# Both products of a mixture-of-experts step as seven block products, the weights' low halves by adding DMAs, and an issue order computed from a graph

## The chip, the core and the metric

The kernel runs on one core of a Trainium2 chip. The metric is the device time of one execution in microseconds (us); the time before is the median of three runs.

## What is computed

A local and global attention makes x (1536 tokens of 512 numbers). Two mixture-of-experts layers follow, both of one form, the first with 4 experts, the second with 8:

```python
for e in range(E):
    h = np.maximum(x @ w1[e], 0.0)          # 512 -> 1024
    out += p[:, e:e + 1] * (h @ w2[e])      # 1024 -> 512
```

In the first layer p comes from an input, normalised over the experts. In the second it comes from `x @ w_gate` by eight rounds of normalising rows and columns (a Sinkhorn iteration), so it is known only some time after that layer has begun.

## The kernel before, in words

**Steps.** The tokens are two blocks of 768, the hidden width of an expert is cut into units of 256: 48 units (16 in the first layer, 32 in the second) times 2 blocks make 96 steps. A step makes a 256 x 768 piece of h from w1 and x (first product), and multiplies it with a 256 x 512 piece of w2 (second product). Every number is a pair of a rounded high half and a low half (`hi`, `lo`), and a product is three matmuls: hi·hi, hi·lo, lo·hi.

**First product** (`product`, L485). It is cut into quadrants and made from seven block products in place of eight, by combinations S1 to S4 of the quadrants of w1 and T1 to T4 of those of x (A11, B21 and so on are the quadrants themselves). A block product is 2 x 3 matmuls of 384 columns, so a step has 42. Partial sums are copied out of PSUM by ACT (L519, L524, L528), later ones added by DVE (L514); ACT makes the rectified high half (L493), DVE the low half (L498).

**Second product** (`g2_tile`, L561 to L563). For each of 6 tiles of 128 tokens, 6 matmuls of 512 columns run into one PSUM bank, 36 in a step. DVE multiplies with p and adds to `acc` in one operation (L581). The result lies with tokens on partitions, so between the layers PE transposes it (`turn_pieces`, L591), and stores of the last step go straight out of `acc` (L585).

**Weights.** One load brings 512 KB of w1 or w2 into `scr`. ACT copies the high halves (L124), POOL subtracts to the low halves (L127) and forms the sums S1 to S4 (L163). There are two sets of weight tiles, a and b.

**Order.** The whole program is written out by hand: `weave` takes pieces of the step's products, the previous step's tiles, the next weights and extra work in the order of strings as STEADY. SP issues all DMAs. Step 0's first product lies inside the attention, as do the first weights (`filler`).

Of the kernel before, what the change touches and what calls it, by code (L numbers as in the profile page):

```python
# [18 lines left out]
def local_global_attention_moe_moe(  # L19
# [46 lines left out]
    ps_x = ctx.enter_context(tc.tile_pool(name="ps_x", bufs=3, space=PSUM))  # L66
    ps_m = ctx.enter_context(tc.tile_pool(name="ps_m", bufs=5, space=PSUM))
# [4 lines left out]
    p1 = const.tile([P, NTT, E1], F32, name="p1")  # L72
# [5 lines left out]
    pp = const.tile([P, NTT, E2], F32, name="pp")  # L78
    rs = const.tile([P, NTT], F32, name="rs")
# [3 lines left out]

# [5 lines left out]

    def new_x(pool, b, c):
        return [pool.tile([P, NOP, HB], F32R, name=f"x{n}{b}{c}") for n in ("hi", "lo")]

    def new_weights(pool, s):
        return {  # L100
            "w1hi": pool.tile([P, NOP, KH, P], F32R, name=f"w1hi_{s}"),
            "w1lo": pool.tile([P, NOP, KH, P], F32R, name=f"w1lo_{s}"),
            "w2hi": pool.tile([P, FC, DM], F32R, name=f"w2hi_{s}"),
            "w2lo": pool.tile([P, FC, DM], F32R, name=f"w2lo_{s}"),
        }

    def new_h(pool, s):
        return [pool.tile([P, FC, BLK], F32R, name=f"{n}_{s}") for n in ("hhi", "hlo")]

    def new_acc(pool, b):  # L110
        return [pool.tile([P, DM], F32, name=f"acc{b}_{t}") for t in range(TPB)]

    xop = {(0, 0): new_x(xp, 0, 0), (0, 1): new_x(xp, 0, 1), (1, 0): new_x(xp, 1, 0)}
    acc = new_acc(xp, 0)
    wsets = [new_weights(xp, "a"), None]
    hsets = [new_h(xp, "a"), None]
# [3 lines left out]
    NU = len(units)  # L120

# [6 lines left out]


    stage = {}  # L130

    def scratch(a, n=KD * FU):
        t = xp.tile([P, 2 * BLK], F32, name="scr", tag="scr", bufs=3)
        return t[:, 0:n].rearrange("x (a c) -> x a c", a=a)

    def load_w1(u):
        layer, e, f = units[u]
        t = stage[u, 1] = scratch(KD)
        w1 = (w1a, w1b)[layer]
        nc.sync.dma_start(  # L140
            out=t, in_=w1[e, :, f * FU:(f + 1) * FU].rearrange("(c p) f -> p c f", p=P)
        )

    def load_w2(u):
        layer, e, f = units[u]
        t = stage[u, 2] = scratch(FC, KD * FU)
        w2 = (w2a, w2b)[layer]
        nc.sync.dma_start(
            out=t, in_=w2[e, f * FU:(f + 1) * FU, :].rearrange("(c p) d -> p c d", p=P)
        )  # L150

# [725 lines left out]
```

## Time and profile before

| | |
|---|---|
| median of three runs | 1630.58 us (1629.75 to 1632.85) |
| the profiled execution's own time | 1632.92 us |
| its span in the trace | 1631.1 us |
| busy share of the span: PE, DVE, ACT, POOL | 98%, 55%, 36%, 35% |
| granted TensorE clock | 0.995 of full speed |

A matmul's recorded duration overlaps the next matmul's; what a matmul costs is read from one start to the next. The same holds for DVE and ACT, whose next operation may start before the recorded end of the one before.

### The profile page before, as it was taken

What the parts mean: (1) busy time and instruction counts of PE and PEld (TensorE: products, weight loads), DVE (VectorE), ACT (ScalarE), POOL (GpSimd) and SP (SyncE); (2) the same over time, 40 slices, a digit from 0 to 9 for tenths busy, and PEclk for the clock granted to TensorE, in tenths of its full rate; (3) what the DMA queues carried; (4) which work ended last, traced back from release to release, by engine and by line L of the source; (5) the groups of instructions that cost most, each with busy time, mean ns of one, the idle gap of its engine ahead of it and who ended that gap; (6) DMA issues with size and microseconds to landing.
All of it is one profiled execution on the core that took longest, in us unless ns stands there. A gap on an engine that the chain in (4) does not pass through costs nothing.

```text
span 1631.1 us, 21762 instructions
## 1 busy us (share of the span) xinstructions
PE 1603.1 (98%) x8515; PEld 1442.1 (88%) x8515; DVE 890.5 (55%) x1524; ACT 580.7 (36%) x1281; POOL 566.0 (35%) x648
## 2 busy tenths in 40 slices
PE   8989999999999998999999999999999999999999
PEld 7878998998999887889999899899998998999987
DVE  7875545545555464377555554554555545545555
ACT  5753333323323345323333333332332333333331
POOL 2743324323333454233432432432333333243240
PEclk9999999999999999999999999999999999999999
DMA  8811110110110001010110011011011011011002
GB/s 190 195 48 44 36 38 26 39 39 27 39 39 27 26 27 52 13 40 27 39 39 27 27 38 39 27 39 39 27 39 39 27 40 39 27 39 39 27 13 78
DMA packets 85032, 70.27 MB, mean 43 GB/s; under 512 B 36032, under 2 KB 71104, under 8 KB 84928
## 3 DMA queue, kind: packets, MB, share of 16 engines
q1 hardware_dynamic: 84928, 68.87, 14.1%
q8 instruction: 67, 1.10, 0.3%
q14 instruction: 37, 0.30, 0.1%
HBM read 64.53 MB, written 3.15 MB: 41 GB/s over the span
## 4 chain that ended last, share of the span: by engine, by line
PE 92%; POOL 3%; DVE 2%; ACT 1%; issue 1%; DMA 0%; SPq 0%; DVEq 0%; POOLq 0%; ACTq 0%
PE px L485 36%; PE pm L561 16%; PE pm L562 16%; PE pm L563 16%; PE pz L485 6%; PE ps L377 1%; POOL xlo L127 1%; PE po L415 1%; POOL scr L603 1%; PE pa L405 0%; POOL scr L163 0%; PE pg L641 0%; ACT xhi L124 0%; DVE xfa L194 0%; POOL w1lo_a L127 0%
## 5 line engine op out<-in xcount | busy, mean ns | idle before, releaser
L581 DVE SCALAR_TENSOR_TENSOR acc<-pm,pp,acc 128x512 f32<-128x512 f32 x347 | 260.4, 751 | 186.7 <-PE pm L563 185.4
L127 POOL TENSOR_TENSOR w1lo_a<-scr,w1hi_a 128x512 fp32r<-128x512 f32 (+1 forms) x144 | 117.6, 837 | 320.2 <-ACT w1hi_a L124 317.1
L514 DVE TENSOR_TENSOR c<-pz,c 128x384 f32<-128x384 f32 x96 | 53.5, 557 | 315.5 <-PE pz L485 311.1
L127 POOL TENSOR_TENSOR w1lo_b<-scr,w1hi_b 128x512 fp32r<-128x512 f32 (+1 forms) x144 | 116.6, 831 | 280.9 <-ACT w1hi_b L124 272.8
L519 ACT COPY c<-px 128x384 f32<-128x384 f32 x96 | 46.1, 481 | 431.7 <-PE px L485 431.7
L485 PE MATMUL px<-xhi,w1hi_a 128*128 128x384 f32 x576 | 196.6, 341 | 3.1 <-ACT c L528 1.4
L485 PE MATMUL px<-xhi,w1hi_b 128*128 128x384 f32 x576 | 194.8, 338 | 2.2 <-ACT c L519 1.0
L485 PE MATMUL px<-xhi,w1lo_a 128*128 128x384 f32 x576 | 194.9, 338 | 0.0
L485 PE MATMUL px<-xlo,w1hi_a 128*128 128x384 f32 x576 | 194.3, 337 | 0.2 <-POOL xlo L127 0.2
L485 PE MATMUL px<-xhi,w1lo_b 128*128 128x384 f32 x576 | 193.8, 337 | 0.0
L485 PE MATMUL px<-xlo,w1hi_b 128*128 128x384 f32 x576 | 193.2, 335 | 0.0
L581 DVE SCALAR_TENSOR_TENSOR acc<-pm,p,acc 128x512 f32<-128x512 f32 x180 | 134.7, 750 | 99.6 <-PE pm L563 99.6
L163 POOL TENSOR_TENSOR scr<-scr 128x256 f32<-128x256 f32 x188 | 140.0, 745 | 11.0
L514 DVE TENSOR_TENSOR c<-px,c 128x384 f32<-128x384 f32 x192 | 106.9, 557 | 45.7 <-PE px L485 45.6
L561 PE MATMUL pm<-w2hi_a,hhi_a 128*128 128x512 f32 x312 | 122.0, 391 | 3.0 <-ACT acc L570 2.0
L561 PE MATMUL pm<-w2hi_b,hhi_b 128*128 128x512 f32 x312 | 122.2, 392 | 0.0
L563 PE MATMUL pm<-w2hi_a,hlo_a 128*128 128x512 f32 x312 | 122.2, 392 | 0.0
L562 PE MATMUL pm<-w2lo_a,hhi_a 128*128 128x512 f32 x312 | 122.0, 391 | 0.0
L562 PE MATMUL pm<-w2lo_b,hhi_b 128*128 128x512 f32 x312 | 122.0, 391 | 0.0
L563 PE MATMUL pm<-w2hi_b,hlo_b 128*128 128x512 f32 x312 | 121.9, 391 | 0.0
L127 POOL TENSOR_TENSOR w2lo_a<-scr,w2hi_a 128x512 fp32r<-128x512 f32 x48 | 61.7, 1306 | 167.9 <-ACT w2hi_a L124 165.9
L127 POOL TENSOR_TENSOR w2lo_b<-scr,w2hi_b 128x512 fp32r<-128x512 f32 x48 | 61.4, 1300 | 166.7 <-ACT w2hi_b L124 166.7
(155 smaller groups left out, 3456.8 us busy)
## 6 DMA issues: line engine op xcount, KB each, us to landing
scr<-in_moe_w_dram SPq DMA_DIRECT2D x96, 512.0 KB, 3.3
vs<-in_v_dram SPq DMA_DIRECT2D x16, 240.0 KB, 3.9
kn<-in_k_dram SPq DMA_DIRECT2D x16, 192.0 KB, 3.3
qn<-in_q_dram SPq DMA_DIRECT2D x16, 192.0 KB, 4.2
vn<-in_v_dram SPq DMA_DIRECT2D x8, 384.0 KB, 3.4
out_dram<-acc SPq DMA_DIRECT2D x12, 256.0 KB, 2.0
vs<-vb SPq DMA_DIRECT2D x8, 144.0 KB
vs<-in_v_dram SPq DMA_DIRECT2D x32, 24.0 KB, 3.7
```

Of the source, the lines that this page charges most:

```text
L127: lo_eng.tensor_tensor(out=lo, in0=src, in1=hi.bitcast(F32), op=ALU.subtract)
L163: sum_eng.tensor_tensor(out=out, in0=x, in1=y, op=op)
L377: nc.tensor.matmul(wide[:, tt], bd[i % 2][:, g * GT + tt].rearrange("x j q -> x (j q)"), kw[i][:, g * GT + tt], start=False, stop=True, sk ...
L415: nc.tensor.matmul(po[j * D:(j + 1) * D, tt * QT:(tt + 1) * QT], vs[i][:, g * GT + tt, j, :], aT[:, tt, j, :], start=True, stop=True,)
L485: nc.tensor.matmul(pm, w[l][:, a, c, :], r[:, x, :], start=first and i == 0, stop=i == n - 1, skip_group_check=True,)
L514: nc.vector.tensor_tensor(out=c, in0=pm, in1=c, op=ALU.add)
L519: nc.scalar.copy(out=c11, in_=px)
L561: nc.tensor.matmul(pm, hhi[:, c, ts], w["w2hi"][:, c, :], start=(c == 0), stop=False)
L562: nc.tensor.matmul(pm, hhi[:, c, ts], w["w2lo"][:, c, :], start=False, stop=False)
L563: nc.tensor.matmul(pm, hlo[:, c, ts], w["w2hi"][:, c, :], start=False, stop=(c == FC - 1))
L581: nc.vector.scalar_tensor_tensor(out=acc[T], in0=pm, scalar=scal, in1=acc[T], op0=ALU.mult, op1=ALU.add)
L603: eng.tensor_tensor(out=out, in0=x, in1=y, op=ALU.subtract)
```

## The change

**Second product.** It too is made from seven block products, of the quadrants of w2 and h and their combinations (`add_second`): per half of the 512 outputs seven block products of 3 matmuls of 384 columns, 42 matmuls in a step. The result lies with tokens on columns, like x. p can no longer be a factor per partition, so it is multiplied into h (`relu`, `PB` is a row of p copied to all partitions through DRAM). The partial results are kept in five accumulators per block and half (m1, m2, z, c12, c22), combined only at the layers' border (`add_turn`) and at the end (`add_out`), where PE now transposes. In the second layer's first expert p is not known yet: those 8 steps leave it out, and `add_scale` multiplies the accumulators later.

**Operands of the second product.** `add_hop` makes the seven combinations of h with four subtractions on DVE, seven high halves on ACT, six low halves on DVE and one on POOL.

**Weights.** w1 and w2 both get S1 to S4 (four sums of 256 columns on POOL each). The low halves are no longer subtracted: ACT writes the negative of the rounded number, and a DMA issued by POOL adds the number to it in SBUF (`accum_op`), three such DMAs for each unit's w1 and w2. The tiles of A11, A12, A22 exist twice, those of S1 to S4 once.

**Order.** Behind the attention every operation is put on a list with what it reads and writes and with a due time; `run_work` issues them by earliest possible start under the table of costs `SPAN`, and by due time among equals. DVE operations with two SBUF inputs and POOL's arithmetic are kept apart there (`port`). The blocks of a unit now always follow each other (b = 0, 1); before, they were exchanged at the border.

```diff
+    SLOT = {A22: 0, A11: 1, A12: 2, S1: 6, S2: 7, S4: 8, S3: 9}
+    NSL = 10
...
+    def slot(u, a):
+        return SLOT[a] + (3 * (u % 2) if SLOT[a] < 3 else 0)
...
-        for c in range(FC):
-            nc.tensor.matmul(pm, hhi[:, c, ts], w["w2hi"][:, c, :], start=(c == 0), stop=False)
-            nc.tensor.matmul(pm, hhi[:, c, ts], w["w2lo"][:, c, :], start=False, stop=False)
-            nc.tensor.matmul(pm, hlo[:, c, ts], w["w2hi"][:, c, :], start=False, stop=(c == FC - 1))
...
-    def relu_lo(S, f, t, c):
-        hhi, hlo = hsets[S[2] % 2]
-        sl = slice(t * HB, (t + 1) * HB)
-        nc.vector.scalar_tensor_tensor(
-            out=hlo[:, f, sl], in0=c, scalar=0.0, in1=hhi[:, f, sl].bitcast(F32),
-            op0=ALU.max, op1=ALU.subtract,
-        )
...
+    def relu(S, out, src, th):
+        if plain(S):
+            nc.scalar.activation(out=out, in_=src, func=AF.Relu)
+        else:
+            nc.vector.scalar_tensor_tensor(
+                out=out, in0=src, scalar=0.0, in1=PB[S[1]][:, th * HB:(th + 1) * HB],
+                op0=ALU.max, op1=ALU.mult,
+            )
...
+            for eng, ids in avail.items():
+                f = free.get(eng, 0.0)
+                for i in ids:
+                    t = max(f, at[i], port) if work[i][5] else max(f, at[i])
+                    key = (t, work[i][3], i)
+                    if best is None or key < best:
+                        best = key
+            t, _, i = best
...
+            aop(lambda: nc.scalar.copy(out=h, in_=src), rd, [key + ("hi",)], due, span)
+            aop(lambda: nc.scalar.mul(l, src, -1.0), rd, [key + ("lo",)], due, span)
+            op(
+                "POOL", "pd", rd, [key + ("lo",)], due + 0.05,
+                lambda: nc.gpsimd.dma_start(out=l, in_=src, accum_op=ALU.add),
+            )
+
+        group(slot(u, A22), 3, 0, wkey(kind, u, A22), start + 0.2, "a768")
...
+        group(6, 2, 0, wkey(kind, u, S1), start + LEAD2, "a512")
+        group(8, 2, 2, wkey(kind, u, S4), start + LEAD2 + 0.1, "a512")
...
+        def one(i, name, due):
+            hi, lo = hop[i][:, 0], hop[i][:, 1]
+            aop(lambda: nc.scalar.copy(out=hi, in_=q[name]), [name], [("hi", i)], due, "ah")
+            eng = "POOL" if i in LOPOOL else "DVE"
+            lo_op(eng, lo, q[name], hi, [name, ("hi", i)], [("lo", i)], due + 0.01)
+
+        def sub(o, x, y, due):
+            vop(lambda: vsub(q[o], q[x], q[y]), [x, y], [o], due)
+
+        one(B11, "q11", d)
+        sub("q12", "q12", "q11", d)
+        one(T1, "q12", d + 0.03)
+        sub("t2", "q22", "q12", d + 0.03)
+        one(T2, "t2", d + 0.1)
+        sub("t4", "t2", "q21", d + 0.1)
+        one(B21, "q21", d + 0.12)
+        one(T4, "t4", d + 0.15)
+        sub("q11", "t2", "q11", d + 0.15)
+        one(B22, "q22", d + 0.2)
+        one(T3, "q11", d + 0.25)
...
+            def fn(cols=cols):
+                s = slot(u, x)
+                for i, (l, r) in enumerate(((hi, 0), (hi, 1), (lo, 0))):
+                    nc.tensor.matmul(
+                        cut[bank], l[:, s, cols], hop[t][:, r],
+                        start=start and i == 0, stop=i == 2, skip_group_check=True,
+                    )
...
+        def copy(out, kout, src, kin, due):
+            aop(lambda: nc.scalar.copy(out=out, in_=src), [kin], [kout], due)
...
+            t, key, bk = acc[b, k, dc], ("acc", b, k, dc), ("bank", bank)
+            if key in fresh:
+                fresh.remove(key)
+                copy(t, key, cut[bank], bk, due)
+            else:
+                vop(lambda: vadd(t, cut[bank], t), [bk, key], [key], due, two=False)
...
+            add_first(n)
+            if b == 1 and u > 0:
+                add_weights(u, 2, n - LEAD)
+            if b == 1 and u + 1 < NU:
+                add_weights(u + 1, 1, n + 1 - LEAD)
+            add_second(n - 1)
+            if n == border:
+                add_turn(0, n + 0.5)
+            if n == border + 1:
+                add_turn(1, n + 0.5)
+            add_hop(n)
...
+            if n == border + 3:
+                add_sinkhorn(n + 0.6)
...
+            if n in (border + 9, border + 10):
+                i = n - border - 9
+                add_scale(i, xf[:, i], n + 0.5)
+        add_second(NS - 1)
...
+        add_out(0, NS + 0.5, stages[0:3], (0, 1, 2, 7))
+        add_out(1, NS + 1.5, stages, tuple(range(8)))
+        run_work()
```

**What the engines issue now.** PE, in the second layer's steady part, before: the first product of a step stands in one piece (`px`, `pz`), then the tiles of the previous step (`pm`).

```order
L485 MATMUL px<-xhi_83,w1hi_b 128x384
L485 MATMUL px<-xlo_84,w1hi_b 128x384
L485 MATMUL px<-xhi_83,w1lo_b 128x384
L561 MATMUL pm<-w2hi_a,hhi_b 128x512
L562 MATMUL pm<-w2lo_a,hhi_b 128x512
L563 MATMUL pm<-w2hi_a,hlo_b 128x512
```

PE at the corresponding place of the change; bank_1552 to 1554 are px, py, pz, bank_1555 to 1558 the second product's four banks, h_1562 to 1568 the operands B11, B21, B22, T1, T2, T3, T4 of the second product.

```order
L509 MATMUL bank_1552<-xlo_84,w1hi 128x384
L509 MATMUL bank_1552<-xhi_83,w1lo 128x384
L758 MATMUL bank_1556<-h_1562,w2hi 128x384 x2
L758 MATMUL bank_1556<-h_1562,w2lo 128x384
L758 MATMUL bank_1558<-h_1565,w2hi 128x384 x2
L758 MATMUL bank_1558<-h_1565,w2lo 128x384
L509 MATMUL bank_1553<-xhi_81,w1hi 128x384
L509 MATMUL bank_1553<-xlo_82,w1hi 128x384
L509 MATMUL bank_1553<-xhi_81,w1lo 128x384
L509 MATMUL bank_1553<-xhi_83,w1hi 128x384
L509 MATMUL bank_1553<-xlo_84,w1hi 128x384
```

Block products of the second product (3 matmuls, L758) now stand between those of the first (6 matmuls, L509).

DVE before, one step: three additions, four low halves, then six accumulations.

```order
L514 TENSOR_TENSOR c_8823<-pz,c_8823 128x384
L514 TENSOR_TENSOR c_8832<-px,c_8832 128x384
L498 SCALAR_TENSOR_TENSOR hlo_a<-c_8823,hhi_a 128x384
L514 TENSOR_TENSOR c_8840<-px,c_8840 128x384
L498 SCALAR_TENSOR_TENSOR hlo_a<-c_8832,hhi_a 128x384
L498 SCALAR_TENSOR_TENSOR hlo_a<-c_8840,hhi_a 128x384
L498 SCALAR_TENSOR_TENSOR hlo_a<-px,hhi_a 128x384
L581 SCALAR_TENSOR_TENSOR acc_0_1538<-pm,pp,acc_0_1538 128x512
L581 SCALAR_TENSOR_TENSOR acc_1_1539<-pm,pp,acc_1_1539 128x512
L581 SCALAR_TENSOR_TENSOR acc_2_1540<-pm,pp,acc_2_1540 128x512
L581 SCALAR_TENSOR_TENSOR acc_3_1541<-pm,pp,acc_3_1541 128x512
```

DVE of the change, about half a step of its 26 operations (q_94 to q_96 are quadrants of h, t_97 and t_98 their combinations, m, z and c the accumulators):

```order
L130 TENSOR_TENSOR z_1573<-bank_1556,z_1573 128x384
L130 TENSOR_TENSOR c_00_1575<-bank_1555,c_00_1575 128x384
L133 TENSOR_TENSOR q_94<-q_94,q_93 128x384
L133 TENSOR_TENSOR t_97<-q_96,q_94 128x384
L523 SCALAR_TENSOR_TENSOR q_95<-bank_1552,pb_1589 128x384
L130 TENSOR_TENSOR c_00_1577<-bank_1558,c_00_1577 128x384
L130 TENSOR_TENSOR m_01_1572<-bank_1556,m_01_1572 128x384
L627 TENSOR_TENSOR h_1565<-q_94,h_1565 128x384
L133 TENSOR_TENSOR t_98<-t_97,q_95 128x384
L627 TENSOR_TENSOR h_1563<-q_95,h_1563 128x384
L130 TENSOR_TENSOR z_1574<-bank_1555,z_1574 128x384
L130 TENSOR_TENSOR c_01_1576<-bank_1557,c_01_1576 128x384
```

Operations that read PSUM (bank) now alternate with operations whose two inputs both lie in SBUF (L133, L627).

POOL before, one unit of two steps:

```order
L127 TENSOR_TENSOR w1lo_b<-scr,w1hi_b 128x512
L127 TENSOR_TENSOR w1lo_b<-scr,w1hi_b 128x256
L163 TENSOR_TENSOR scr<-scr 128x2x128 x2
L127 TENSOR_TENSOR w1lo_b<-scr,w1hi_b 128x256
L163 TENSOR_TENSOR scr<-scr 128x2x128 x2
L127 TENSOR_TENSOR w1lo_b<-scr,w1hi_b 128x256 x3
L127 TENSOR_TENSOR w2lo_b<-scr,w2hi_b 128x512 x2
```

POOL of the change, one unit (raw_91 and raw_92 hold w1 and w2):

```order
L627 TENSOR_TENSOR h_1568<-t_98,h_1568 128x384
L657 TENSOR_TENSOR raw_92<-raw_92 128x256 x4
L650 DMA w1lo<-raw_91 128x768
L657 TENSOR_TENSOR raw_91<-raw_91 128x256 x4
L650 DMA w2lo<-raw_92 128x512
L627 TENSOR_TENSOR h_1568<-t_98,h_1568 128x384
L650 DMA w2lo<-raw_92 128x512
L650 DMA w1lo<-raw_91 128x512 x2
L650 DMA w2lo<-raw_92 128x768
```

Eight subtractions to low halves have become six DMAs, the sums have doubled to eight, and POOL takes one low half of h in each step.

## Rows read from the trace of the kernel before

**Rows 1.** The page: busy time of each engine, and the granted clock in 40 slices.
```profile
PE 1603.1 (98%) x8515; PEld 1442.1 (88%) x8515; DVE 890.5 (55%) x1524; ACT 580.7 (36%) x1281; POOL 566.0 (35%) x648
...
PEclk9999999999999999999999999999999999999999
```

**Rows 2.** The page: the chain that ended last, by engine.
```profile
PE 92%; POOL 3%; DVE 2%; ACT 1%; issue 1%; DMA 0%; SPq 0%; DVEq 0%; POOLq 0%; ACTq 0%
```

**Rows 3.** Stages, cut where pz starts in steps 4, 28, 40, 95: busy us (instructions), clock.
```profile
110.70:163.40 52.70, 50.79 (x257) 45.26 (x254) 33.08 (x56) 17.84 (x37) 20.04 (x21) 1.00 0.11 37
163.40:536.10 372.70, 372.70 (x1874) 338.07 (x1874) 194.07 (x312) 123.19 (x264) 122.72 (x144) 1.00 0.11 35
536.10:752.20 216.10, 209.44 (x1069) 183.11 (x1068) 120.03 (x240) 83.56 (x177) 86.44 (x88) 0.99 0.09 29
752.20:1606.60 854.40, 854.40 (x4291) 774.70 (x4291) 448.87 (x722) 281.75 (x603) 279.36 (x326) 1.00 0.10 33
1606.60:1631.10 24.50, 20.73 (x98) 17.54 (x96) 12.59 (x19) 2.49 (x5) 0.00 (x0) 0.96 0.35 129
```

**Rows 4.** Timeline of PE in a steady step: start us, duration, line, tiles.
```profile
1000.82 0.34 PE L485 MATMUL pz<-xhi,w1hi_a 128*128 128x384 f32 x1
...
1001.86 0.34 PE L485 MATMUL px<-xhi,w1hi_a 128*128 128x384 f32 x1
...
1005.00 0.40 PE L561 MATMUL pm<-w2hi_b,hhi_b 128*128 128x512 f32 x1
...
1013.20 0.33 PE L485 MATMUL px<-xhi,w1hi_a 128*128 128x384 f32 x1
...
1016.34 0.33 PE L485 MATMUL pz<-xhi,w1hi_a 128*128 128x384 f32 x1
```

**Rows 5.** Timeline of DVE: operations that follow each other at once.
```profile
1003.17 0.56 DVE L514 TENSOR_TENSOR c<-px,c 128x384 f32<-128x384 f32 x1 [0.48 <-PE px L485]
1003.64 0.55 DVE L498 SCALAR_TENSOR_TENSOR hlo_a<-c,hhi_a 128x384 fp32r<-128x384 f32 x1
...
115.78 1.14 DVE L194 TENSOR_TENSOR scr<-scr 128x384 f32<-128x384 f32 x2
```

**Rows 6.** All groups by form: POOL, and ACT (busy us, mean ns, idle before).
```profile
L163 POOL TENSOR_TENSOR scr<-scr 128x256 f32<-128x256 f32 x188 | 140.0, 745 | 11.0
...
L603 POOL TENSOR_TENSOR scr<-scr 128x384 f32<-128x384 f32 x8 | 8.5, 1089 | 0.0
...
L519 ACT COPY c<-px 128x384 f32<-128x384 f32 x96 | 46.1, 481 | 431.7 <-PE px L485 431.7
L124 ACT CAST w2hi_b<-scr 128x512 fp32r<-128x512 f32 x48 | 27.3, 618 | 0.0
L124 ACT CAST xhi<-scr 128x768 fp32r<-128x768 f32 x14 | 11.7, 839 | 24.2 <-POOL scr L603 14.9 <-DVE scr L194 7.2 <-POOL xlo L127 1.3
```

**Rows 7.** Timeline of DVE and of POOL at one moment of the layers' border.
```profile
595.83 1.88 DVE L498 SCALAR_TENSOR_TENSOR hlo_b<-c,hhi_b 128x384 fp32r<-128x384 f32 x1 [4.67 <-ACT hhi_b L493]
...
595.45 1.85 POOL L127 TENSOR_TENSOR xlo<-scr,xhi 128x768 fp32r<-128x768 f32 x1 [0.95 <-ACT xhi L124]
```

**Rows 8.** The page's DMA issues: KB each, median us to landing.
```profile
scr<-in_moe_w_dram SPq DMA_DIRECT2D x96, 512.0 KB, 3.3
...
out_dram<-acc SPq DMA_DIRECT2D x12, 256.0 KB, 2.0
```

**Rows 9.** Timeline: PE and SP, one issue of a load; the last row is DVE's.
```profile
110.70 0.50 PE L561 MATMUL pm<-w2hi_a,hhi_a 128*128 128x512 f32 x1
...
1008.86 0.37 SPq L140 DMA_DIRECT2D scr<-in_moe_w_dram  x1
...
1627.37 0.75 DVE L581 SCALAR_TENSOR_TENSOR acc<-pm,pp,acc 128x512 f32<-128x512 f32 x1 [0.61 <-PE pm L563]
```

**Rows 10.** All groups by form: gate logits and transposes on PE, the iteration's widest operation on DVE.
```profile
L591 PE MATMUL pxt<-ident,acc 128*128 128x128 f32 x48 | 7.8, 272 | 0.0
...
L641 PE MATMUL pg<-xhi,wghl 128*16 128x384 f32 x20 | 7.1, 355 | 0.0
...
L675 DVE TENSOR_TENSOR pp<-pp,rs 128x96 f32<-128x96 f32 x8 | 3.3, 418 | 0.3
```

More of the change, by code (lines that the diff above doesn't have):

```diff
@@ new lines, in run_work @@
+    def run_work():
+        n = len(work)
+        after = [[] for _ in range(n)]
+        left = [len(w[2]) for w in work]
+        for i, w in enumerate(work):
+            for j in w[2]:
+                after[j].append(i)
+        at = [0.0] * n
+        free = {}
+        avail = {}
+        port = 0.0
+        for i in range(n):
+            if not left[i]:
+                avail.setdefault(work[i][0], []).append(i)
+        for _ in range(n):
+            best = None
+            for eng, ids in avail.items():
[6 more added lines that the diff above has]
+            t, _, i = best
+            eng, (busy, late), _, _, fn, shared = work[i]
+            avail[eng].remove(i)
+            free[eng] = t + busy
+            if shared:
+                port = t + busy
+            fn()
+            for j in after[i]:
+                same = work[j][0] == eng
+                at[j] = max(at[j], t + busy if same else t + late + HOP_WAIT)
+                left[j] -= 1
+                if not left[j]:
+                    avail.setdefault(work[j][0], []).append(j)
+        work.clear()
@@ new lines, in vop, with aop, lo_op, fn @@
+    def vop(fn, reads, writes, due, span="v", two=True):
+        op("DVE", span, reads, writes, due, fn, two)
+    def aop(fn, reads, writes, due, span="a"):
+        op("ACT", span, reads, writes, due, fn)
+    def lo_op(eng, out, src, hi, reads, writes, due, n=1):
+        def fn(e=nc.gpsimd if eng == "POOL" else nc.vector):
+            e.tensor_tensor(out=out, in0=src, in1=hi.bitcast(F32), op=ALU.subtract)
+        span = ("p384", "p768")[n - 1] if eng == "POOL" else ("v", "v768")[n - 1]
+        op(eng, span, reads, writes, due, fn, True)
@@ L847, in local_global_attention_moe_moe @@
-        for _ in g2_tiles(steps[-1]):
-            pass
+        ps = ctx.enter_context(tc.tile_pool(name="ps", bufs=1, space=PSUM))
+        full = [ps.tile([P, 512], F32, name=f"bank{i}") for i in range(8)]
+        cut = [t[:, 0:HB] for t in full]
+        banks += [3, 4, 5, 6]
+        spare = full[7]
+        xop[1, 1] = new_x(wb, 1, 1)
+        for i in range(NOP):
+            hop[i] = wb.tile([P, 2, HB], F32R, name=f"h{i}")
+        for b in range(2):
+            for k in KEYS:
+                for c in range(KH):
+                    acc[b, k, c] = wb.tile([P, HB], F32, name=f"{k}_{b}{c}")
+                    fresh.add(("acc", b, k, c))
```

838 lines of the change are left out of this document (522 added, 316 removed), and 5 rows, old and new, of the table SPAN.

## The prediction, made before the changed kernel ran

> **What bounds the kernel now.** I read the page's busy times first: PE is busy for 98% of the span, no other engine for more than 55%, and the granted clock is 9 tenths or more, the 2.4 GHz level, in every slice [rows 1]. The chain that ended last runs through PE for 92% [rows 2]. So PE's own matmuls set the time, and the question is how many us of them a step has. The stages give it: from step 4 to step 28 it is 372.70/24 = 15.53 us, from 40 to 95 it is 854.40/55 = 15.53 us, with PE busy all through [rows 3]. The timeline splits it: 36 matmuls of 512 columns take 1013.20 - 1005.00 = 8.20 us, and 6 of 384 columns take 1001.86 - 1000.82 = 1.04 us, 0.173 each; 42 of these are 7.28 us, and with a few slower starts 7.33 [rows 4]. Outside the steady steps the kernel loses little: the 12 steps at the border take 216.10 us, 29.7 over 12 x 15.53, of which PE has 6.7 idle, and the entry into the steps and the end lose about 3 and 4 us (52.70 and 24.50 us, less the matmuls in them) [rows 3].
>
> **What the change removes on PE.** The second product goes from 36 matmuls of 512 columns to 42 of 384: 8.20 us become 7.28, as a block product's 0.173 us per matmul already includes loading new weights for each. A step is then 2 x 7.28 = 14.56 us where nothing waits, 0.97 less. For 95 steps that is -92.2, and -0.9 for step 0's second product: **-93 us**. A PE that waits gives this back, so the rest is about waits.
>
> **DVE.** It has 26 operations of 384 columns in a step, where it had 13. One follows another after 0.47 us, and a pair in which the second needs the first takes 1.14 us in place of 1.03 [rows 5]. I count four such pairs in a step's rows: 26 x 0.47 + 4 x 0.11 = 12.7 us. That is 87% of 14.56: covered, with 1.9 us to spare, where before DVE was busy for 448.87 of 854.40 us [rows 3].
>
> **The port that DVE and POOL share.** This is the dearest unknown. A DVE operation with two SBUF inputs took 1.88 us in place of 0.55 when a POOL operation was under way: it started at 595.83, POOL's ran from 595.45 to 597.30, and it ended 0.41 later; it had stood still until POOL was done [rows 5, 7]. In the change 12 of DVE's 26 operations have two SBUF inputs (4 subtractions, 6 low halves, 2 of the multiplications with p). POOL holds the port for (8 x 0.745 + 2 x 1.089)/2 = 4.1 us of a step [rows 6]. Bounds: nothing, if each POOL operation falls beside PSUM reads, and 4.1 us, if all of it stops DVE (12.7 + 4.1 = 16.8). With 12 of 26 at the head of the queue when POOL starts, some 12/26 of 4.1 = 1.9 us, or a little more, are to be expected without an order; the new order keeps the two apart. I take 1 us: DVE 13.7, PE still slower. The Trainium skill's page "SBUF — State Buffer", section "Who interferes with whom", says the same as a rule: the pair is locked for a whole instruction and the second comer fully blocks. Rows 7 agree. By the rule alone, with no luck from the order, DVE would need some 15 us and pace the step; that is the first rival.
>
> **PE's waits in a step.** In the new order the PSUM bank px is used four times in a step, and twice it is written again soon after DVE must have read it: three short block products, 1.56 us, lie between. DVE's operation started 0.27 us behind such a product's end (1003.17 - 1001.86 - 1.04) and takes 0.56 [rows 4, 5]; with some 0.2 to tell PE, an estimate, about half a us is left. A POOL operation stands in the way in 4.1/14.6 = 28% of cases and then costs some 0.3 us beyond the slack. That is 2 x 0.28 x 0.3 = 0.15 us a step: **+14 us**; bounds 0 and 0.4 a step (38).
>
> **ACT, weights and SP.** ACT gets 14 copies of about 0.48 us a step and, per unit, 4 of 0.84 and 8 of 0.62 [rows 6]: 6.7 + 4.2 = 10.9 of 14.56, covered. POOL's six DMA issues per unit have no row: an issue on SP took 0.37 us [rows 9]; at most (29.1 - 8.2)/6 = 3.5 us each fit. I take 1, nearer the row: POOL has 7 of 14.56. How long an adding DMA takes to land has no row either. It moves 256 or 384 KB and reads both sides; a store of 256 KB landed in 2.0 us, a load of 512 KB in 3.3 [rows 8]. Bounds 2.0 and, with reading twice 384 KB behind another transfer, 7; I take 4.5. What it must fit into: S1 and S2 of w2 exist once. Between the last matmul that reads them for one unit and the first for the next, the new order has 4 block products of 1.04 and 7 of 0.52 us = 7.8 us; ACT's two writes take 1.6 with their waits, so the add has 6.1. Covered, at 0. The Trainium skill's page "DMA: Bandwidth & Descriptors", section "Anatomy of one DMA — SWDGE (gpsimd) path", gives a fit of 2.0 us and bytes/436 KB per us, so 2.6 to 2.9 us here as an estimate; by it the window is never at risk. No row here shows it.
>
> **Attention, entry.** Up to the first tile of the second product nothing changes in kind (110.70 us, [rows 9]), but POOL gets 8 more operations of 0.745 us there, beside the ones that attention waits for: +3 us (0 to 8). Behind it step 0's h needs 10 DVE operations and x's last part 8, while PE has only 7.3 us to do: +2 over the 3 lost now (-1 to 6).
>
> **Border.** Gone are 48 transposes there [rows 10]; they come back at the end. The turn costs DVE 22 operations a block, the later scaling 16: 76 x 0.47 = 36 us in a stage where DVE has 1.9 us spare a step, or 3.7 in the 8 steps that leave p out. It also still has the iteration's small operations, 64 in number (3.3 us for the widest eight, rows 10; some 18 in all). Work 12 x 12.7 - 8 x 1.9 + 36 + 18 = 191 us, against PE's 12 x 14.56 + 7 for the gate = 182. So 9 us over 182 if it packs perfectly, some 30 if not, and the gate's 7 [rows 10] in both; as the work comes in bursts I take 26 + 7 = 33 over the steps in place of 29.7, **+3** (-12 to +20).
>
> **End.** Before, the last operation on DVE starts 0.4 us behind PE [rows 9]. Now the last second product has no first product to hide its copies behind (some 4 us), 48 transposes of 0.11 us come in (5), and three combinations, a copy and a store follow (7 in place of 4): **+12** (6 to 20).
>
> **Sum** on the profiled span: 1631.1 - 93 + 14 + 3 + 2 + 3 + 12 = 1572; its own time was 1.8 us above its span and 2.3 above the median of the runs shown, so I predict a median of **1572 us**. With the terms at their lower ends 1540, with a few at their upper ends 1595.
>
> **Rivals.**
> - *DVE paces the steps.* Its place is the steady step; DVE needs 12.7 plus some 2.3 us of standing behind POOL, 15.0. For: rows 7, and 87% use without it. Against: the order puts PSUM reads beside POOL's work. 95 x (15.0 - 14.71) = +28: **1600**, 1590 to 1640. The loss begins where DVE stands still for more than 1.9 us a step, and the gain is gone at 2.6 (15.33 us a step).
> - *Slower: the adding DMAs come late.* Place: S1 to S4 of w2, once per unit. If an add takes longer than 6.1 us from issue to landing, PE waits for the rest 47 times. The gain of 59 us is gone at 7.3 us; at 8 it is +89: **1661**. For: POOL issues in order, an add waits behind sums and other adds, and none has a row. Against: 2.0 and 3.3 us [rows 8].
> - *The matmuls are not cheaper.* 384 columns in 0.173 is 0.451 ns a column, 512 in 0.228 is 0.445 [rows 4], so the short ones lose nothing. Were weight changes dearer in the new mixture, at 0.182 us each the step would be 15.3 and the time that of before.
> - *Everything fits.* No waits, a good border: **1535**.
>
> **Chances.** My forecast (1543 to 1590) 0.64; DVE paces 0.20, of it 0.02 slower than before; adds late 0.09; no change to speak of 0.03; everything fits 0.04. A difference of 0.2%, 3 us, is about what runs of this kernel can tell. Faster 0.64 + 0.18 + 0.04 = 0.86, same 0.03, slower 0.11. The range 1543 to 1626 leaves out the 0.04 below and 0.14 above.
>
> **What would show it.** Right: PE's steps 14.6 to 14.9 us apart, PE over 96% busy, DVE over 85% in the steady stage, adds landing within 6 us, 210 us or so for the 12 border steps, some 10 us between the last matmul of a step and the end. Wrong: PE waiting for DVE in every step with DVE never idle (first rival), or for w2's tiles once in two steps (second); a border or an end that costs 20 us more than I give it.

## The result, and the profile after

The changed kernel takes 1644.03 us (median of 5 runs, 1640.3 to 1648.5), the kernel before 1630.70 in the same session: the ratio is 1.0078, 95% interval 1.0056 to 1.0101. It is slower by 0.8%, where 1572 us, 3.6% faster, was predicted.

The page of the profiled execution (span 1642.3 us), its busy times and three lines of its 40 slices, against [rows 1]:

```profile
PE 1559.0 (95%) x9098; PEld 1496.6 (91%) x9098; DVE 1497.1 (91%) x2770; ACT 1060.6 (65%) x2222; POOL 735.3 (45%) x849
...
PE   7889999999999988898899999999999999999998
...
DVE  6877999899999997888999999999999999999998
...
PEclk9999999999999999998999999999999999999999
```

PE does its work in less time, but it now pauses: 95% busy where it was 98%, and DVE has gone from about half to 91%. The windows below are the stages of the steps (a step is counted as 84 matmuls of the two products; step 4 starts at 175.8, step 31 at 583.6, step 43 at 821.6, step 94 at 1597.9), against [rows 3]:

```profile
175.80:583.60 407.80, 401.09 (x2269) 391.49 (x2268) 382.83 (x704) 264.89 (x540) 188.04 (x219) 1.00 0.47 101
583.60:821.60 238.00, 209.23 (x1095) 194.44 (x1094) 203.15 (x405) 155.90 (x330) 98.75 (x108) 0.93 0.37 80
821.60:1597.90 776.30, 759.61 (x4286) 739.35 (x4286) 735.46 (x1326) 502.07 (x1019) 349.43 (x405) 1.00 0.48 102
```

The columns are the stretch and its length, busy us (and instructions) of PE, PE's weight loads, DVE, ACT and POOL, then granted clock, DMA share and GB/s. The 27 steps before the border take 15.10 us each and the 51 behind it 15.22; the forecast was 14.71. The mean hides a pattern: two neighbouring steps, a unit, in the same view.

```profile
1262.20:1277.70 15.50, 14.99 (x86) 14.47 (x85) 14.96 (x27) 9.62 (x20) 9.61 (x12) 1.00 0.36 69
1277.70:1292.30 14.60, 14.60 (x86) 14.60 (x86) 12.75 (x27) 10.55 (x21) 3.58 (x5) 1.00 0.57 126
```

One step of a unit runs bare, that is without waits, the other loses about 1.2 us (over the 51 steps the two kinds take 14.61 and 15.86). In the losing one POOL is busy for 9.61 us and DVE for 14.96 of 15.50; in the bare one POOL for 3.58 and DVE for 12.75. The prediction can now be set against the trace stage by stage. Put together by stage, its terms make 1570 us, 2 less than its own sum of 1572:

```
stage                         predicted                          measured   difference
up to step 4                  113.7 + 51.0 + 3 + 2   = 169.7      175.8       +6.1
27 steps                      27 x 14.71             = 397.2      407.8      +10.6
12 steps at the border        174.7 + 33             = 207.7      238.0      +30.3
51 steps                      51 x 14.71             = 750.2      776.3      +26.1
last 2 steps and the end      29.1 + 4 + 12          =  45.1       44.4       -0.7
```

In the first line 113.7 is 110.70 with the 3 us given to attention, and 51.0 is what PE has left of four steps when attention ends (294 matmuls of 0.173). So the steady steps lack 37 us and the border 30. The experiments are about these two.

What DVE does in the 51 steps, by group (count, busy us, mean ns, idle before), is next to [rows 5] the view that counts:

```profile
L627 DVE TENSOR_TENSOR h<-q,h 128x384 fp32r<-128x384 f32 x255 | 160.6, 630 | 0.0
L130 DVE TENSOR_TENSOR m<-bank,m 128x384 f32<-128x384 f32 x205 | 112.1, 547 | 1.9 <-PE bank L758 1.9
L130 DVE TENSOR_TENSOR c<-bank,c 128x384 f32<-128x384 f32 x204 | 107.3, 546 | 1.0 <-PE bank L758 1.0
L523 DVE SCALAR_TENSOR_TENSOR q<-q,pb 128x384 f32<-128x384 f32 x101 | 65.2, 646 | 3.5
...
L627 DVE TENSOR_TENSOR h<-t,h 128x384 fp32r<-128x384 f32 x51 | 55.7, 1092 | 0.0
L133 DVE TENSOR_TENSOR q<-t,q 128x384 f32<-128x384 f32 x51 | 52.1, 1022 | 0.0
```

Operations that read a PSUM bank last 546 ns as before; those with two SBUF inputs last 630 to 1092. All that exceeds 0.56 us lies in operations that overlap a POOL operation with two SBUF inputs: 191 of them with 88 us of standing, 1.73 us a step. By the POOL operation under way, T4's low half (the one low half of h that POOL makes) accounts for 1.05 of it and the weight sums for 0.68. It lies unevenly: 2.45 us in a losing step, 1.03 in a bare one. The first of two places where PE loses, seen in a timeline (start, duration, engine; idle before and its releaser in brackets):

```profile
1260.66 3.39 POOL L657 TENSOR_TENSOR raw<-raw 128x256 f32<-128x256 f32 x4 [3.23 <-issue]
...
1261.98 0.56 DVE L130 TENSOR_TENSOR q<-bank,q 128x384 f32<-128x384 f32 x1 [0.64 <-PE bank L509]
...
1262.57 0.88 DVE L523 SCALAR_TENSOR_TENSOR q<-q,pb 128x384 f32<-128x384 f32 x1
...
1263.48 0.98 DVE L133 TENSOR_TENSOR q<-q,q 128x384 f32<-128x384 f32 x1
...
1264.38 0.54 DVE L130 TENSOR_TENSOR q<-bank,q 128x384 f32<-128x384 f32 x1
...
1264.98 0.44 PE L509 MATMUL bank<-xhi,w1hi 128*128 128x384 f32 x1 [0.51 <-DVE q L130]
```

Four sums run in a row on POOL. Two DVE operations in a row, 0.88 and 0.98 in place of 0.55, stand behind them; the third, which must empty a bank, starts late by both, and PE waits 0.51 us for that bank. In front of the run DVE had been idle for 0.64 us: it carried no backlog in. This is the place that the prediction priced at 0.15 us a step.

The second place comes later in the losing step, here in the next unit:

```profile
1302.90 2.03 DVE L627 TENSOR_TENSOR h<-q,h 128x384 fp32r<-128x384 f32 x1
...
1303.20 1.31 POOL L627 TENSOR_TENSOR h<-t,h 128x384 fp32r<-128x384 f32 x1
...
1305.33 0.54 DVE L627 TENSOR_TENSOR h<-q,h 128x384 fp32r<-128x384 f32 x1
...
1305.92 0.44 PE L758 MATMUL bank<-h,w2hi 128*128 128x384 f32 x1 [0.68 <-DVE h L627]
```

Here T4's low half is on POOL; a DVE operation that meets it takes 2.03 us, and PE waits 0.68 us for an operand h that DVE makes two operations later. By the distances between PE's starts, the bank makes 14.3 of the 33.7 us that the 51 steps lose and the operand h 12.4. In 18 of the 25 losing steps DVE stands for 0.9 us or more behind T4's low half, and they lose 0.88 us each in their later part; in the other 7 it stands for 0.5, and they lose 0.12 there.

The adding DMAs do what was expected of them (KB, us to landing), and PE waits 2.3 us for them in the whole run:

```profile
L758 PE MATMUL bank<-h,w2lo 128*128 128x384 f32 x1344 | 452.0, 336 | 2.3 <-DMA w2lo<-raw 2.3
...
w1lo<-raw POOLq DMA_DIRECT2D x94, 256.0 KB, 3.9
w2lo<-raw POOLq DMA_DIRECT2D x94, 256.0 KB, 3.3
w1lo<-raw POOLq DMA_DIRECT2D x47, 384.0 KB, 3.8
w2lo<-raw POOLq DMA_DIRECT2D x47, 384.0 KB, 4.4
```

### The profile page after: what moved, and what is told of

Its sections match the earlier page's. It is cut to its first block, busy times and chain, and to the rows that moved or that the text cites. A ratio compares the mean times of both kernels' runs of the same rounds, so it can differ in the third digit from the quotient of the medians.

```text
span 1642.3 us, 26636 instructions
## 1 busy us (share of the span) xinstructions
PE 1559.0 (95%) x9098; PEld 1496.6 (91%) x9098; DVE 1497.1 (91%) x2770; ACT 1060.6 (65%) x2222; POOL 735.3 (45%) x849
## 4 chain that ended last, share of the span: by engine, by line
PE 34%; DVE 17%; issue 2%; DMA 1%; ACT 0%; DVEq 0%; SPq 0%; ACTq 0%; POOLq 0%
PE bank L509 17%; PE bank L758 17%; DVE q L133 3%; DVE h L627 3%; DVE q L523 3%; DVE c L130 2%; DVE q L130 2%; DVE m L130 2%; DVE z L130 1%; DVE t L133 1%; DVE z L133 0%; DMA raw<-in_moe_w_dram 0%; DMA w1lo<-raw 0%; DVE c L136 0%; PE bank L1050 0%
## 5 line engine op out<-in xcount | busy, mean ns | idle before, releaser
L758 PE MATMUL bank<-h,w2hi 128*128 128x384 f32 x2688 | 702.6, 340 | 19.4 <-DVE h L627 12.0
L758 PEld LDWEIGHTS bank<-h,w2hi 128*128 128x128 f32 x2688 | 482.7, 189 | 43.6 <-DVE h L627 21.5
L509 PE MATMUL bank<-xhi,w1hi 128*128 128x384 f32 x1330 | 455.1, 342 | 23.7 <-DVE q L130 17.0
L758 PE MATMUL bank<-h,w2lo 128*128 128x384 f32 x1344 | 452.0, 336 | 2.3 <-DMA w2lo<-raw 2.3
L509 PE MATMUL bank<-xlo,w1hi 128*128 128x384 f32 x1330 | 450.6, 339 | 1.9 <-DVE xlo L627 1.6
L509 PE MATMUL bank<-xhi,w1lo 128*128 128x384 f32 x1330 | 449.2, 338 | 0.0
L657 POOL TENSOR_TENSOR raw<-raw 128x256 f32<-128x256 f32 x376 | 315.5, 839 | 283.0 <-issue 127.3
L627 DVE TENSOR_TENSOR h<-q,h 128x384 fp32r<-128x384 f32 x480 | 299.4, 627 | 6.9 <-ACT h L727 5.9
L509 PEld LDWEIGHTS bank<-xhi,w1hi 128*128 128x128 f32 x1330 | 253.3, 190 | 38.1 <-DVE q L130 28.6
L509 PEld LDWEIGHTS bank<-xlo,w1hi 128*128 128x128 f32 x1330 | 253.3, 190 | 4.6 <-DVE xlo L627 3.7
L758 PEld LDWEIGHTS bank<-h,w2lo 128*128 128x128 f32 x1344 | 253.9, 189 | 2.7 <-DMA w2lo<-raw 2.6
L509 PEld LDWEIGHTS bank<-xhi,w1lo 128*128 128x128 f32 x1330 | 253.3, 190 | 0.0
L627 POOL TENSOR_TENSOR h<-t,h 128x384 fp32r<-128x384 f32 x96 | 121.7, 1268 | 36.8 <-ACT h L727 31.7
```

Of the source, the lines that this page charges most:

```text
L509: nc.tensor.matmul(pm, l[:, s, cs_], r[:, x, :], start=first and i == 0, stop=i == n - 1, skip_group_check=True,)
L627: e.tensor_tensor(out=out, in0=src, in1=hi.bitcast(F32), op=ALU.subtract)
L657: lambda o=o, f=f, x=x, y=y: nc.gpsimd.tensor_tensor(out=r[:, o], in0=r[:, x], in1=r[:, y], op=f),
L758: nc.tensor.matmul(cut[bank], l[:, s, cols], hop[t][:, r], start=start and i == 0, stop=i == 2, skip_group_check=True,)
```

## The experiments

All are edits of the changed kernel, timed in three rounds beside the kernel before. In the table "27", "12" and "51" are what the three stages lose over bare steps of 14.56 us in the profiled execution, and "stand" is DVE's time above 0.56 us an operation, per step of the 51.

```
run                     median    ratio to before (95%)     27     12     51   stand
the change             1644.03   1.0078 (1.0056, 1.0101)   14.7   63.2   33.7   1.73
e1_no_sums             1583.26   0.9701 (0.9680, 0.9721)    0.6   49.9    1.7   0.89
e2_lo_dve              1636.53   1.0028 (1.0017, 1.0038)   11.3   71.2   20.4   0.96
e3_m2_act              1649.80   1.0114 (1.0090, 1.0138)   17.7   68.0   34.2   1.69
e4_both                1634.60   1.0014 (1.0002, 1.0026)   12.7   73.1   19.5   1.01
e5_spread              1644.35   1.0082 (1.0061, 1.0103)   14.0   66.0   33.2   1.18
e6_spread_dve          1649.32   1.0107 (1.0090, 1.0124)   24.3   61.9   36.0   1.25
e7_no_border           1629.85   0.9985 (0.9974, 0.9997)   17.7   51.9   28.2   1.64
e8_turn_dve            1645.40   1.0080 (1.0055, 1.0106)   15.4   66.2   28.2   1.61
e9_quarters            1835.92   1.1244 (1.1225, 1.1262)   81.6   70.7  152.5   0.48
e10_quarters_spread    1672.69   1.0238 (1.0220, 1.0256)   29.9   70.3   45.8   0.44
e11_p128               1654.18   1.0138 (1.0110, 1.0166)   19.7   64.5   35.1   1.61
e12_p128_spread        1626.85   0.9966 (0.9954, 0.9978)   15.9   69.5   13.0   0.60
e13_one_iteration      1638.50   1.0035 (1.0022, 1.0047)   18.1   59.5   29.7   1.69
e14_scale_later        1627.24   0.9964 (0.9946, 0.9982)   14.8   64.7   16.3   0.64
e15_adds_and_iteration 1618.53   0.9907 (0.9892, 0.9923)   14.1   43.1   29.4   1.64
e16_p128_m2_act        1650.91   1.0143 (1.0115, 1.0171)   12.7   62.1   27.1   1.24
e17_p128_lo_dve        1654.85   1.0141 (1.0124, 1.0158)   19.4   71.6   34.7   1.16
```

**What the sums cost.**

In add_weights:

```diff
-                lambda o=o, f=f, x=x, y=y: nc.gpsimd.tensor_tensor(
-                    out=r[:, o], in0=r[:, x], in1=r[:, y], op=f
-                ),
+                lambda: None,
```

> Leaves out POOL's sums of weight quarters (8 per unit; the products then use wrong sums); every other instruction keeps its place in the order. Port theory: DVE's operations with two SBUF inputs stand still behind POOL, and the sums lie all in the second step of a unit, whose 15.86 us then fall to 14.6 to 14.8: 47 x 1.1 = about 50 us less, 1590 to 1605. Rival (DVE paces by the number of its operations, or PE waits on banks, whoever holds the port): within 10 us of 1644.

61 us less, and the steady steps are bare: 14.58 and 14.59 us on average. The 14.56 of the prediction holds. DVE in the same 51 steps of this run:

```profile
L627 DVE TENSOR_TENSOR h<-q,h 128x384 fp32r<-128x384 f32 x255 | 139.5, 547 | 0.0
...
L627 DVE TENSOR_TENSOR h<-t,h 128x384 fp32r<-128x384 f32 x51 | 73.3, 1437 | 0.0
...
L133 DVE TENSOR_TENSOR q<-t,q 128x384 f32<-128x384 f32 x51 | 28.6, 560 | 0.0
```

One operation still stands for 0.89 us in every step, behind T4's low half on POOL, and PE loses nothing by it; in the change the same low half costs PE the second of its two places. So standing as such is not the price: where it falls is, and without the sums it falls where there is room. The number of DVE's operations is not the price either, as it is the same 26 here. The border gets 13 us better too.

**More or less work for DVE.**

```diff
-    LOPOOL = (T4,)
+    LOPOOL = ()
```

> T4's low half of h on DVE in place of POOL. Port theory: that POOL operation makes DVE stand still for 1.05 us a step and costs DVE itself 0.47, so DVE gains 0.58 a step; in the steps that DVE paces that comes off the time: 25 to 35 us less, 1610 to 1620. Rival (the number of DVE's operations paces): 27 in place of 26, up to 0.47 a step more, 1644 to 1666.

```diff
-    M2ACT = False
+    M2ACT = True
```

> The accumulation of m2 through ACT and PE (two copies in place of one DVE addition, per output chunk): DVE has 24 operations a step, ACT 4 more copies, about 13 us of 14.6. Port theory and the rival by number both: DVE has 0.94 a step more room, the second step's loss of 1.2 goes mostly: 1595 to 1615. A third theory (ACT's copies, not DVE, are what PE waits for): slower than 1644 by 10 us or more.

With both edits:

> e2 and e3 together: 25 operations on DVE and no T4 on POOL. Port theory: no steady step waits for DVE, 1590 to 1605, with what is left lost in the entry, at the border and at the end. By number alone: 1615 to 1630. ACT as the bound: above 1644.

None of the three came out within a range stated for it. e2 went the way of the port theory, by 7.5 us where 25 to 35 were expected: the steady steps gained 17, the border lost 8. e3 took two operations from DVE and gained nothing, but does not tell why: in its 51 steps PE's waits for DVE fall from 29 us to 17, and 15 us of waits for ACT's copies and the adding DMAs come in, where the change has 1. e4 gains as much as e2, and shows one thing more: in its losing steps (15.34 us) DVE is busy for 14.25, less than a bare step lasts, and PE still waits 11 us for it in the 51 steps. Room on DVE over a step does not cover a stall.

**Where the sums lie.**

In add_weights (in e6 the key is w2's S1 low half, wkey(2, u - 1, S1) + ("lo",)):

```diff
+        behind = [("lo", T4)] if kind == 1 else []
-                "POOL", "p256", [R[x], R[y]], [R[o]], start + 0.5,
+                "POOL", "p256", [R[x], R[y]] + behind, [R[o]], start + 0.5,
```

> The sums of w1's quarters stand behind T4's low half on POOL, so that w1's four sums fall in the first step of a unit and w2's four in the second; nothing is added or removed. Port theory, with the concentration as the cause: each step now has about 1.0 us of standing behind T4 and 0.7 behind sums, 1.7, less than the room DVE has in 14.56; both steps 14.6 to 14.9, steady loss 47 falls to 10 to 15: 1605 to 1615. Rival: it is the total that costs, wherever it lies: 1638 to 1648.

> The sums spread as in e5, and all low halves of h and x on DVE (T4's, and three of seven per block and chunk in the entry and the turn). Port theory: 27 operations, 13.2 us, and 0.7 of standing a step: fits in 14.56, steady loss below 8; at the border six POOL operations of 1.27 less to stand behind against six of 0.47 more: 1595 to 1610. Rival by number of DVE operations: slower than e5.

The loss stayed (33.2 for 33.7), but the theory of concentration was not tested by it. The sums of w1 and w2 start some 11 us apart where it was 7, and DVE's standing fell from 1.73 to 1.18 a step; yet it fell in the step that lost nothing (1.03 to 0.13), and the losing step kept 2.28 of its 2.45 us, now all behind the sums. Inside that step the loss moved: PE's wait for the bank is gone, that for the operand h, now behind the second group of sums, grew from 12 us to 18, and 8 us go to another bank. e6, with a DVE operation more, is slower by 5 us, as its rival by number said; e1 speaks against that rival.

**How long a POOL operation is.**

The sums and POOL's low halves call this in place of one operation:

```diff
+    def in_pieces(out, x, y, f):
+        w = out.shape[-1] // 4
+        for i in range(4):
+            c = slice(i * w, (i + 1) * w)
+            nc.gpsimd.tensor_tensor(out=out[..., c], in0=x[..., c], in1=y[..., c], op=f)
```

> POOL's operations with two SBUF inputs behind the attention (the sums, T4's low half, the turn's) each cut into four of a quarter of the columns; same work, same order. Theory of local lateness: what costs PE is that one DVE operation waits for the rest of a long POOL operation; it now waits 0.25 us at most: DVE's standing falls from 1.73 us a step to 0.7 or less, the steady loss of 47 to 5 to 15, some of the border's goes too: 1590 to 1605. Rival (POOL keeps the port as long as it has operations queued, or the total counts): 1640 to 1660.

> e9 with the sums placed as in e5. Local lateness: where the sums lie matters little once they are short: within 6 us of e9, 1585 to 1605. Rival as for e9: 1640 to 1660.

e9's expectation is right on the cause and far off on the time. Standing fell to 0.48 us a step, and PE's waits for DVE were all but gone. But POOL became slow; POOL's timeline in a losing step:

```profile
1405.48 0.87 POOL L659 DMA_DIRECT2D w1lo<-raw  x1
1409.43 6.05 POOL L623 TENSOR_TENSOR raw<-raw 128x64 f32<-128x64 f32 x16 [3.08 <-issue]
1415.43 0.85 POOL L659 DMA_DIRECT2D w2lo<-raw  x1
```

On the page, the row of the matmuls that waited (busy, mean ns, idle before):

```profile
L765 PE MATMUL bank<-h,w2lo 128*128 128x384 f32 x1344 | 472.5, 352 | 157.0 <-DMA w2lo<-raw 157.0
```

Four sums in pieces take 6.05 us where they took 3.4 (the last section takes this apart). w2's adding DMA stands behind w1's sums in POOL's queue, so it is issued late, and PE waits 157 us in all. This is the prediction's second rival, with its mechanism as told, brought about by the edit. In e10 w1's sums stand behind that DMA; the wait is gone and another is left, PE for an ACT copy (63 us) that stands behind a weight copy that waits for the last sum.

Pieces of 128 columns, in the change's order and in e5's:

```diff
-        w = out.shape[-1] // 4
-        for i in range(4):
-            c = slice(i * w, (i + 1) * w)
+        for i in range(0, out.shape[-1], 128):
+            c = slice(i, i + 128)
```

> As e9, but pieces of 128 columns: two for a sum, three for a low half. In e9 POOL needed 0.37 us for 64 columns and as much for 96, and its queue then held back w2's adding DMAs (PE waited 157 us for them), while PE's waits for DVE were gone. Pieces of 128 should take 0.40 to 0.45, so that four sums need 3.4 us as before and the DMAs are not late. Theory of local lateness: a DVE operation waits 0.4 us at most, standing falls from 1.73 us a step to about 0.9, the steady loss from 47 to 10 to 25: 1605 to 1622. Rival (the total counts): 1640 to 1650. Late DMAs again: over 1660.

> Pieces of 128 columns and w1's sums behind T4 as in e5 and e10. In e10 PE waited 1.5 us a unit for an ACT copy that stood behind a weight copy waiting for w1's last sum; with the sums 1 us shorter a third to a half of that should be left: 1610 to 1630. Rival (the total counts): 1640 to 1650.

e11 missed its range: short pieces in the old order cut the standing behind the sums only from 0.68 to 0.51, and PE waits 19 us for w2's DMAs. In e12 pieces and order together do what neither does alone: 51 steps lose 13.0, standing is 0.60, and the kernel takes 1626.85 us, 17 less than the change and 0.34% less than the kernel before (interval 0.22 to 0.46%). Its window over the 51 steps, in which PE is busy for 753.65 of 755.60 us (759.61 of 776.30 in the change):

```profile
828.90:1584.50 755.60, 753.65 (x4287) 741.01 (x4286) 686.77 (x1327) 504.86 (x1021) 406.74 (x711) 1.00 0.48 105
```

And the DVE group that stood longest in the change, now at 555 ns for 1092:

```profile
L635 DVE TENSOR_TENSOR h<-t,h 128x384 fp32r<-128x384 f32 x51 | 28.3, 555 | 2.0 <-ACT h L734 0.2
```

**The border.**

In add_turn, and likewise in add_scale:

```diff
-                vop(lambda: f(out, x, y), [kx, ky], [ko], d)
+                vop(lambda: None, [kx, ky], [ko], d)
```

> Leaves out DVE's additions and subtractions of the turn and its scaling at the border (60 operations; the values are then wrong), order otherwise kept. If the border's 64 us of loss are DVE's: 28 us of work and 3 to 6 of standing go, and PE's gaps with them: 1608 to 1616. If they are the iteration's chain, the gate or the copies on ACT: at most 10 us less, 1634 to 1644.

In add_turn, three times:

```diff
-            one(T1, b12, k12, "POOL", due + 0.02)
+            one(T1, b12, k12, "DVE", due + 0.02)
```

> The turn's low halves that POOL makes (6) on DVE. Port theory: DVE's operations in the turn all have two SBUF inputs and stand behind POOL's 1.27 us each; on DVE they cost 0.47: 3 to 6 us less, 1638 to 1641. By number of DVE operations: 3 us more.

In add_sinkhorn, and so for each operation of a round:

```diff
-        for _ in range(8):
+        for it in range(8):
...
-            tv(lambda: nc.vector.reciprocal(out=rs, in_=rs), ["rs"], ["rs"])
+            tv(lambda it=it: it or nc.vector.reciprocal(out=rs, in_=rs), ["rs"], ["rs"])
```

> Leaves out seven of the iteration's eight rounds at the border (56 small DVE operations and 7 PE round trips); order otherwise kept. The border loses 64 us over bare steps. If the iteration's chain holds up PE: the steps in which it lies (7.9, 4.1 and 1.7 us lost) become bare, 10 to 14 us less, 1630 to 1635. If DVE's long additions are the border and the iteration lies beside: at most 5 less.

> e7 and e13 together: neither the 60 additions and scalings nor seven of eight rounds. If the border's loss is DVE's work (of either kind) and the clock that falls behind PE's idle stretches: 64 falls to 25 to 35, with the gate's matmuls (7), the low halves and the sums' own 8 left: 1608 to 1618. If something else holds PE there (the gate's bank, ACT's copies): 1622 or more.

In e12's add_scale:

```diff
-                vop(lambda: f(out, x, y), reads, [ko], due)
+                vop(lambda: f(out, x, y), reads, [ko], due + c * 0.9)
```

> e12 with the second chunk's scaling due 0.9 of a step later, so that DVE's 32 scaling operations are not two blocks of 16 in a row. If PE's long idle stretches there (5.8 and 4.7 us) and the half-clock stretches behind them are the price, the steps 40 and 41 lose 4 to 9 us less: 1618 to 1624. If only DVE's amount of work counts: within 3 us of e12's 1627.

e7 brought the border from 63.2 to 51.9, less than half of what was expected, and e13 to 59.5; together, e15, 43.1, more than the two summed. So DVE's long operations and the iteration cover for each other, and 20 of the 63 us are theirs; 25 to 35 were to be left, and 43 are. The sums alone bring 13 (e1), and whether these come on top of the 20 was not run. e8 saved nothing. e14 moved the loss without making it less: steps 40 to 43 take 75.5 us in both e12 and e14, which fits that DVE's amount of work counts there and not its coming in one piece, though no run changed the amount alone. What the rest of e15's 43 us is made of was not taken apart further; the gate's matmuls are 7 of it.

**What limits e12.**

e16 is e12 with e3's edit, e17 is e12 with e2's edit and e6's key.

> e12 with m2's accumulation through ACT and PE (as e3): 24 operations on DVE, ACT 4 copies more a step. If DVE's lack of room is what e12 still loses in its steady steps (28 us over bare), 10 to 20 of it go: 1607 to 1617. If ACT's order is what is left (PE waited 23 us of weight loading for an ACT copy in e12): 1627 to 1640, with ACT's copies the last wait.

> e12 with T4's low half on DVE (as e2), w1's sums behind w2's first adding DMA: DVE 27 operations, nothing of T4 on POOL. If room on DVE is what is left: 0.47 more, against no more than 0.1 of standing behind T4 in e12, so 10 to 30 us slower than e12's 1627. If POOL's queue (weights' sums and DMAs late) is what is left: 3 us less in each unit's POOL queue, 1615 to 1627.

Both are slower than e12. e17 moved the sums a little with the key, and PE waits at the h of the second group again (27 us for DVE). e16's profiled execution was the quickest of its runs (1634, the others 1649 to 1660), so its profile does not explain its median. Of the 13.0 us that e12's 51 steps lose in its profile, 7.5 are waits for banks that DVE's accumulations empty and 4.1 waits for ACT's copies; why these are late stays open.

## Why the prediction was wrong, point by point

- **The matmuls.** Right. Bare steps take 14.56 us, in every second step of the change and in nearly all steady steps of e1, 0.97 less than before, as predicted.
- **DVE's operations.** Right: 26 a step, 0.47 apart.
- **The port and PE's waits, the step that failed.** PE's waits were given 0.15 us a step (at most 0.4), on the ground that a POOL operation in the way costs "some 0.3 us beyond the slack" at one bank, where "about half a us is left", and the rest of DVE's standing was to be covered by its spare 1.9 us. Measured are 0.62 us a step. Three parts of the step failed.
  - *The slack.* In the losing step the operation that empties the bank is third in DVE's queue, and in 22 of the 25 such steps PE's loss there is the standing of the two in front less 0.07 us, to within 0.01. So the slack was 0.07 us and nearly every stall passed on to PE; in the order of the other step DVE is done 0.8 us before PE needs the bank. (No run shows the 0.2 us to tell PE: from the recorded end on DVE to PE's start it is 0.054 to 0.057 us in 75 of 77 waits.)
  - *The place.* The operand h, late behind T4's low half, has no term in the prediction; it makes 12.4 of the 33.7 us in the 51 steps.
  - *The averages.* "The loss begins where DVE stands still for more than 1.9 us a step" was put against an average of 1 us; it was 1.73, but 2.45 in the losing steps. By that rule these would lose 0.55 us each; they lose 1.30. So the average over a unit was wrong, and spare time over a step is not the cover that counts: e4 has it and loses.

  e1 shows the cause: without the sums the loss is 0.03 a step, with 0.89 us of standing in a place that has slack. The lock itself is as [rows 7] showed it, and as the Trainium skill has it ("SBUF — State Buffer", section "Who interferes with whom": the pair is held for a whole instruction). The trace agrees: only operations beside a POOL instruction stand, and e9's shorter instructions make them stand for less.
- **The first rival, DVE paces the steps.** The nearest of the cases, right in engine and port, wrong in its price: it let nothing be lost below 1.9 us of standing a step, and by it the losing steps would lose 0.55 of the 1.30 us that they do. DVE as a whole does not pace the steps (26 operations and bare steps in e1, room and a loss in e4); a few of its operations do.
- **The adding DMAs.** Right: 3.3 to 4.4 us to landing against the estimate of 4.5, an issue 0.87 to 0.90 against 1, and no wait to speak of. The Trainium skill's fit for such a path ("DMA: Bandwidth & Descriptors", section "Anatomy of one DMA — SWDGE (gpsimd) path") gave an estimate of 2.6 to 2.9; here the trace differs, and the measured 3.3 to 4.4 holds. The second rival did not happen here; e9 shows that 2.6 us more on POOL's queue bring it about.
- **The border.** Sized at 33 us over bare steps, measured 63. By the distances between PE's starts in the 12 steps, 35.7 us are waits of PE, where 26 were given for packing; 13.6 are gate, folding and iteration on PE, where 7 were given for the gate; and 13.4 are matmuls that start 0.2 to 0.36 us apart, most of them at the lower clock behind PE's waits, a term that the sum lacked. These three excesses, 9.7, 6.6 and 13.4, are the 30 us.
- **Entry.** 14 us lost up to step 4 (175.8 less 110.7 and 51.0) in place of 3 + 3 + 2: attention ends 1.5 us later, and step 0's h comes late, so that the first tile of the second product starts at 120.65 us.
- **End.** Right: 15.3 us over two bare steps, 4 + 12 predicted.

## What to carry to other kernels

Spare time of an engine over a step is no cover for a stall: look up, for the operation that is held up, how long until its result is needed, and put against that the longest run of stalls that can stand in front of it. An order computed from a graph holds only as far as its durations and its rule for the shared port do; two queues that meet there each go on when they can, not when the plan says. To cut long operations of the engine that holds the port shortens the stalls, but every piece has a fixed cost and every cut lets the other engine in; it helps only where that engine's own queue has room, so the two have to be changed together.

## What the hardware showed beside this

**A cut costs POOL a fixed part, and lets DVE in.** In e9 POOL's operations of 64 columns start 0.28 us apart where no DVE operation with two SBUF inputs is in the way (0.275 to 0.289 in 398 cases); with 96 columns it is 0.35, with 128 in e12 0.42, and in the kernel before 0.70 with 256 and 1.25 with 512. That is about 0.145 us for an operation and 2.15 ns for a column. Beside such a DVE operation POOL stands too: the mean of 64 columns is then 0.45, up to 0.67. A piece of e9 beside DVE, and four that nothing disturbs:

```profile
1096.28 0.55 DVE L636 TENSOR_TENSOR h<-q,h 128x384 fp32r<-128x384 f32 x1
1096.33 0.68 POOL L623 TENSOR_TENSOR raw<-raw 128x64 f32<-128x64 f32 x1
...
1099.29 1.16 POOL L623 TENSOR_TENSOR raw<-raw 128x64 f32<-128x64 f32 x4
```

So the 16 pieces of four sums would take 4.5 us alone; the rest of e9's 6 is POOL standing behind DVE. The 0.37 that e11's expectation names for a piece of e9 is this mixture.

**DVE reading PSUM does not stand.** In the change's 51 steps 216 operations that read a bank beside a POOL addition lasted 548 ns, 318 alone 549. And 57 operations with two SBUF inputs beside nothing but POOL's issue of a DMA lasted 549: the issue did not hold them up.

**PE pays for a wait twice.** At the border PE waits for DVE, which has scaling operations in front, and then runs at a lower clock. PE's rows in one such place:

```profile
763.99 0.34 PE L758 MATMUL bank<-h,w2lo 128*128 128x384 f32 x1
769.80 0.69 PE L509 MATMUL bank<-xhi,w1hi 128*128 128x384 f32 x1 [5.47 <-DVE q L130]
...
770.61 0.52 PE L509 MATMUL bank<-xhi,w1lo 128*128 128x384 f32 x1
770.93 0.52 PE L509 MATMUL bank<-xhi,w1hi 128*128 128x384 f32 x1
```

The windows of 5 us, with the columns as above:

```profile
765.00:770.00 5.00, 0.20 (x1) 0.20 (x2) 4.96 (x8) 0.00 (x0) 3.87 (x4) 0.71 0.01 2
770.00:775.00 5.00, 5.00 (x19) 5.00 (x20) 4.50 (x10) 0.46 (x1) 0.00 (x0) 0.60 0.00 2
775.00:780.00 5.00, 5.00 (x31) 5.00 (x30) 3.44 (x8) 3.84 (x9) 0.88 (x1) 1.00 0.14 26
```

Behind 5.5 us of waiting the matmuls start 0.32 us apart in place of 0.17, the 1.2 GHz level, up to 773.5; the granted clock of those 5 us is 0.60. Eleven such distances, 0.15 us too long each, are an estimate of 1.6 us more for the wait of 5.5.
